# Linear attention in front of a low-rank mixer: transposes by token halves, scores in one run, outputs on the whole array

## The chip, the cores and the metric

The kernel runs on one core of one Trainium2 chip. The metric is the device time of one execution in microseconds. The kernel before was timed three times: 671.49, 671.64 and 671.76 us, median 671.64 us.

## What is computed

Two blocks, one after the other. The first is linear attention with decay ("lightning attention") over 4 batches, 8 heads, 768 tokens and 64 dimensions; the second is a mixer on its output.

```python
# attention, by blocks of tokens (block = 64 in the reference)
intra = einsum('bhic,bhjc->bhij', qb, kb) * Dmask        # Dmask[i,j] = lam**(i-j) for i >= j
intra = einsum('bhij,bhjd->bhid', intra, vb)
inter = einsum('bhid,bhde->bhie', qb * lam_pow, kv_state)
out   = intra + inter
kv_state = lam**block * kv_state + einsum('bhsd,bhse->bhde', kb * rev_pow, vb)
# x = out as (batch, tokens, 512), then the mixer
h = x.transpose(0, 2, 1) @ U @ V                         # U: 768 x 32, V: 32 x 768
u = x + h.transpose(0, 2, 1)
y = u + maximum(u @ w_ch1, 0) @ w_ch2                    # w_ch1: 512 x 2048, w_ch2: 2048 x 512
```

All is fp32. The reference's block of 64 tokens is a way to write the sum; the kernel uses blocks of 128, which gives the same result.

## The kernel before

The tokens are cut into 24 steps (`NS`) of 128 tokens, six (`NT`) to a batch. A step `s` has number `c = s % NT` in its batch. The kernel has two parts: a front, in which attention and the mixing over tokens are done step by step, and the two large products (`hidden`, L719 to 749, and `product`, L857 to 870), which take u in 512-token groups. The front ends at about 119 us in the profile.

What one step of the front does on TensorE (PE):

- `prep` (L360) with `turn_half` (L347): q and k of 128 tokens arrive as 128 tokens x 8 heads x 64. Four transposes each on the whole 128x128 array bring them to "two heads x 64 dimensions" on the partitions and tokens along the row. ScalarE (ACT) copies each set of four from PSUM (L358). Step 0 does this in two parts.
- `scores` (L394): per head, k times q over 64 dimensions, for 128 x 128 tokens. Heads of a pair sit on the lower and upper 64 partitions, so two row tiles (64x128) work side by side; after step 6 (`s > NT`) the key tokens are halved as well, and four 64x64 tiles work side by side.
- `masked` (L405): VectorE (DVE) multiplies the scores by the decay mask, in two instructions of 128x512, into `sm`.
- `intra` (L446): the masked scores times v, per head, by halves of the tokens on 128x64 column tiles, into `px`; then ACT copies `px` to `x_nat` (L459).
- `inter` (L431): q scaled by GpSimd (POOL, L383) times the state `kv`, on 64x64 tiles, into the same `px`. It opens the sum in `px`, except at the first step of a batch, which has no state.
- `state` (L411): scaled k (POOL, L372) times v on 128x64 tiles into `pkv`; DVE adds the faded state (L426). The last step of a batch has none.
- `low` (L464): after the six steps of a batch, x times U on 128x32 tiles; `low_rows` (L477) splits the result into a part with few bits and its rest.
- `mix` (L512): seven steps later (`done = s - NT - 1`), one 512-column product adds the mixed part; DVE adds it to x (L518).
- `turn` (L523): four transposes of u for the large products. DVE splits them (L537 and L548), a closure `turned` in the next step does the rest on ACT (L551) and POOL (L552). The u tile itself is stored to HBM from here (L535) for the residual at the end.

The order of all this is written out by hand in the list `pieces` (L562 to 584), and the tile framework is told to keep it (`manual_schedule`). In one pass of the loop for step `s`, TensorE gets: q and k transposes of step `s + 1`, `mix(done)`, `low` if a batch has ended, `intra(s)`, `state(s)`, `scores(s + 1)`, `inter(s + 1)`, and `turn(done)`. Weight steps for the large products (`aside`, `late`) are set among them on DVE, ACT and the DMA queue of SyncE. q, k and v are loaded ahead, into three or four buffers each, as soon as a step has let go of one (`load_next`).

PSUM in the front has eight banks: one each for `pq`, `pk`, `pt` and `pu`, two for the scores and two for `px`. `pkv` uses the bank of `pk`, the output transposes that of `pt`, the mix and the first low-rank product that of `pu`.

An fp32 matmul stands in the trace as two records (two passes, each with its own weight load); a transpose and a matmul of the float32r type as one.

Of the kernel before, what the change touches and what calls it, by code (L numbers as in the profile page):

```python
# [18 lines left out]
def kernel(  # L19
# [319 lines left out]
    def keep_busy(n):  # L339

        out = one_bank([P, C], "idle", "pq")
        for i in range(n):
            nc.tensor.matmul(out=out[:, 0:P], lhsT=blank, rhs=blank, start=True, stop=True)  # L343

    qts, kts = {}, {}

    def turn_half(s, a0, name):  # L347

        ts, tag = (qts, ("pq", "pt")) if name == "q" else (kts, ("pk", "pu"))
        if a0 == 0:  # L350
            ts[s] = att.tile([P, HP, P], FP32, tag=name + "t", bufs=2, name=name + "t")
        n = HP // parts(s)
        pt = one_bank([P, n, P], "p" + name, tag[a0 > 0])
        for a in range(a0, a0 + n):
            nc.tensor.transpose(  # L355
                out=pt[:, a - a0, :], in_=raw[s, name][:, 2 * a : 2 * a + 2, :], identity=ident
            )
        nc.scalar.copy(ts[s][:, a0 : a0 + n, :], pt)  # L358

    def prep(s):  # L360
        for a0 in range(0, HP, HP // parts(s)):
            for name in "qk":
                turn_half(s, a0, name)
        st[s].update(qt=qts.pop(s), kt=kts.pop(s))
        for name in "qk":
            load_next(name)
# [27 lines left out]
    def scores(s):  # L394
        qt, kt = st[s]["qt"], st[s]["kt"]
        st[s]["pss"] = pss = two_banks("pss", "pss").rearrange("p x (a i) -> p x a i", a=HP)
        for a in range(HP):
            for x in range(2):
                for rows in half if s > NT else [slice(0, P)]:
                    nc.tensor.matmul(  # L400
                        out=pss[rows, x, a, :], lhsT=kt[half[x], a, rows],
                        rhs=qt[half[x], a, :], start=True, stop=True,
                    )

# [6 lines left out]
    def state(s):  # L411
        c = s % NT
        if c < NT - 1:
            ks, vr = st[s]["ks"], raw[s, "v"]
            pkv = one_bank([P, HP, D], "pkv", "pk")
            for a in range(HP):
                for x in range(2):
                    nc.tensor.matmul(  # L418
                        out=pkv[half[x], a, :], lhsT=ks[:, a, x, :], rhs=vr[:, 2 * a + x, :],
                        start=True, stop=True,  # L420
                    )
            kv[s + 1] = att.tile([P, HP, D], FP32, tag="kv", bufs=2, name="kv")
            if c == 0:
                nc.vector.tensor_copy(out=kv[s + 1], in_=pkv)
            else:
                nc.vector.tensor_tensor(out=kv[s + 1], in0=pkv, in1=st[s]["faded"], op=ALU.add)  # L426
        del st[s]
        del raw[s, "v"]
        load_next("v")

    def inter(s):  # L431

        st[s]["px"] = both = two_banks("px", "px")
        px = both[:, :, 0 : HP * D].rearrange("p x (a e) -> p x a e", a=HP)
        if s % NT == 0:
            return

        for a in range(HP):
            for x in range(2):
                for t in range(2):  # L440
                    nc.tensor.matmul(  # L441
                        out=px[half[t], x, a, :], lhsT=st[s]["qs"][half[x], a, half[t]],
                        rhs=kv[s][half[x], a, :], start=(a == 0), stop=False,
                    )

    def intra(s):  # L446
        first = s % NT == 0
        sm, vr, px = st[s]["sm"], raw[s, "v"], st[s]["px"]
        px = px[:, :, 0 : HP * D].rearrange("p x (a e) -> p x a e", a=HP)
        for a in range(HP):  # L450
            for x in range(2):
                for t in range(2):
                    nc.tensor.matmul(  # L453
                        out=px[half[t], x, a, :], lhsT=sm[:, x, a, half[t]],
                        rhs=vr[:, 2 * a + x, :], start=(first and a == 0), stop=(a == HP - 1),
                    )
        pool, tag = (att, "x10") if s % 10 == 5 else (x_pool, "x")
        xs[s] = pool.tile([P, C], FP32, tag=tag, name="x_nat")
        nc.scalar.copy(xs[s].rearrange("p (a x e) -> p x a e", a=HP, x=2), px)  # L459


    pps = {}

    def low(b):  # L464

        tag = "pq" if b else "pu"
        pp = one_bank([P, P], "pp", tag) if b < B - 1 else bank([P, P], "pp", "b2")
        for c in range(NT):
            for g in range(G):
                nc.tensor.matmul(  # L470
                    out=pp[g * R : (g + 1) * R, :], lhsT=u_w[:, c, :],
                    rhs=xs[b * NT + c][:, g * P : (g + 1) * P],
                    start=(c == 0), stop=(c == NT - 1),
                )
        pps[b] = pp

    def low_rows(b):  # L477
# [3 lines left out]
        own = [(slice(g * R, (g + 1) * R), slice(g * P, (g + 1) * P)) for g in range(G)]  # L481
        if b == 0:

            rows_f = tmp("p_f")[0:R]
            for rows, cols in own:
                nc.scalar.copy(rows_f[:, cols], pp[rows])
            own = [(slice(0, R), slice(0, C))]
            pp = rows_f
        for rows, cols in own:
# [19 lines left out]
    def next_of_low(b):  # L509
        pps[b].pop(0)()  # L510

    def mix(s):  # L512
        b, c = divmod(s, NT)
        pu = one_bank([P, C], "pu", "pu") if s < NS - NT - 1 else bank([P, C], "pu", "b2")
        nc.tensor.matmul(  # L515
            out=pu, lhsT=v_hl[:, c * P : (c + 1) * P], rhs=p_hl, start=True, stop=True
        )
        nc.vector.tensor_tensor(out=xs[s], in0=pu, in1=xs[s], op=ALU.add)  # L518

    uhl, ud, turned = {}, {}, {}  # L520
    hl_at, d_at = [hl_pool], [d_pool]

    def turn(s):  # L523
# [5 lines left out]
        cols = slice(n * P, (n + 1) * P)  # L529
        pt = one_bank([P, CT, P], "put", "pt") if g < FG else bank([P, CT, P], "put", "b1")  # L530
        for ct in range(CT):
            nc.tensor.transpose(  # L532
                out=pt[:, ct, :], in_=xs[s][:, ct * P : (ct + 1) * P], identity=ident
            )
        nc.sync.dma_start(out=u_d[s], in_=xs.pop(s))  # L535
        t = tmp("ut").rearrange("p (c n) -> p c n", n=P)
        nc.vector.tensor_scalar(t.bitcast(U32), pt.bitcast(U32), HI, None, ALU.bitwise_and)  # L537
        hi, low, diff = uhl[g][:, 0, :, cols], uhl[g][:, 1, :, cols], ud[g][:, :, cols]
        if g >= FG:

            nc.vector.scalar_tensor_tensor(diff, t, 1.0 + E, pt, ALU.mult, ALU.subtract)
# [5 lines left out]

        nc.vector.tensor_tensor(out=low, in0=pt, in1=t, op=ALU.subtract)  # L548

        def rest():  # L550
# [3 lines left out]
            )  # L554

        turned[s] = rest

    pieces = [("prep", 0), ("scale", 0), ("scores", 0), ("inter", 0), ("masked", 0)]  # L562
    for s in range(NS):
        b, c = divmod(s, NT)
        done = s - NT - 1
        more = s + 1 < NS
        step = [("prep", s + 1), ("scale", s + 1)] * more + [("fade", s)] * (c == 1)
        step += [("late", s - 1)] * (s in (NT, 3 * NT - 1))
        step += [("mix", done)] * (0 <= done < NS - NT - 1)
        step += [("low", b - 1)] * (c == 0 and b > 0)  # L570
        step += [("low_rows", b - 1)] * (c == 0 and b > 0)
        step += [("intra", s)]
        step += [("next_of_low", b - 1)] * (c == 0 and b > 0)
        step += [("late", s)] * (s < NT - 1 or s == NT) + [("state", s)]
        step += [("next_of_low", b - 1)] * (c == 0 and b > 0)
        step += [("turned", done - 1)] * (done > 0) + [("late", s)] * (done >= 0)
        step += [("next_of_low", b - 1)] * (c == 0 and b > 0)
        step += [("scores", s + 1)] * more
        step += [("aside", s)] * (s >= 2 * NT)
        step += [("inter", s + 1), ("masked", s + 1)] * more  # L580
        step += [("fade", s + 1)] * (more and c > 0)
        step += [("aside", s)] * (s < 2 * NT)
        step += [("turn", done)] * (done >= 0 and done // TG < FG)
        pieces += step
    waiting = {name: list(range(NS)) for name in "qkv"}

    def load_next(name, engine=nc.sync):
# [6 lines left out]
        "intra": intra, "state": state,  # L594
        "low": low, "low_rows": low_rows, "next_of_low": next_of_low, "mix": mix, "turn": turn,
        "scale": scale, "turned": lambda s: turned.pop(s)(),
    }
# [77 lines left out]
    for name in "qkv":  # L675
        load_next(name)
    make_identity(nc, ident)
    keep_busy(2)
    pl = one_bank([P, H], "pl", "pt")
    nc.tensor.matmul(out=pl, lhsT=lam_row[:, H:], rhs=lam_row[:, 0:H], start=True, stop=True)  # L680
# [289 lines left out]
```

## Time and profile before

| What | Value |
|---|---|
| median of 3 runs | 671.64 us |
| the profiled execution's own time | 671.76 us |
| its span on the core | 669.9 us |
| q and k transposes, L355 | 192 records, 284 and 279 ns mean |
| scores on 64x128 tiles, L400 | 112 records, 305 ns mean |
| scores on 64x64 tiles, L400 | 544 records, 276 ns mean |
| outputs, L453, on 128x64 tiles | 768 records, 225 ns mean |
| state, L418 | 320 records, 222 ns mean |
| state's part, L441 | 640 records, 220 ns mean |
| output transposes in all, L532 | 96 records, 282 ns mean |
| mix in all, L515 | 24 records, 451 ns mean |
| masking, L409 on DVE | 48 instructions, 685 ns mean |

How to read it: a record's length holds its latency, and matmuls overlap in the pipeline, so the mean of one is not what one costs. What counts is the distance from the start of one row of the timeline to the start of the next. The clock of TensorE is granted in full after the opening.

The shapes in a row of the profile are "tile rows * tile columns" and then the moving operand, "partitions x elements".

### The profile page before, as it was taken

What the parts mean: (1) busy time and instruction counts of PE and PEld (TensorE: products, weight loads), DVE (VectorE), ACT (ScalarE), POOL (GpSimd) and SP (SyncE); (2) the same over time, 40 slices, a digit from 0 to 9 for tenths busy, and PEclk for the clock granted to TensorE, in tenths of its full rate; (3) what the DMA queues carried; (4) which work ended last, traced back from release to release, by engine and by line L of the source; (5) the groups of instructions that cost most, each with busy time, mean ns of one, the idle gap of its engine ahead of it and who ended that gap; (6) DMA issues with size and microseconds to landing.
All of it is one profiled execution on the core that took longest, in us unless ns stands there. A gap on an engine that the chain in (4) does not pass through costs nothing.

```text
span 669.9 us, 13328 instructions
## 1 busy us (share of the span) xinstructions
PE 663.9 (99%) x5204; PEld 544.5 (81%) x5204; DVE 497.5 (74%) x873; ACT 277.5 (41%) x517; POOL 112.1 (17%) x92
## 2 busy tenths in 40 slices
PE   9999999999999999999999999999999999999997
PEld 8898989788888888888888888888888888888886
DVE  4689989877999777777797265787586775865864
ACT  4675866454655444444454122232322322322320
POOL 4455767240000000000000000030030300300300
PEclk9999999999999999999999999999999999999999
DMA  8999894354776655555577989854363353543421
GB/s 188 219 234 248 212 246 141 102 196 153 262 251 233 215 202 202 201 202 204 204 282 273 326 308 392 282 184 136 95 220 95 118 196 95 160 155 94 163 90 63
DMA packets 131776, 131.29 MB, mean 196 GB/s; under 512 B 81346, under 2 KB 89794, under 8 KB 131714
## 3 DMA queue, kind: packets, MB, share of 16 engines
q1 hardware_dynamic: 130512, 130.05, 61.1%
q8 instruction: 41, 0.67, 0.4%
q10 hardware_dynamic: 1202, 0.39, 0.2%
q14 instruction: 21, 0.17, 0.1%
HBM read 80.09 MB, written 50.33 MB: 195 GB/s over the span
## 4 chain that ended last, share of the span: by engine, by line
PE 97%; DVE 1%; DMA 1%; ACT 0%; issue 0%; DVEq 0%; ACTq 0%
PE pz L733 27%; PE pz L868 13%; PE pz L866 13%; PE pd L743 13%; PE pd L870 13%; PE px L453 4%; PE pss L400 3%; PE put L532 2%; PE pq L355 2%; PE pkv L418 1%; PE pk L355 1%; PE px L441 1%; DMA qraw<-in_q_dram 1%; PE pp L470 1%; PE pu L515 1%; PE idle L343 0%
## 5 line engine op out<-in xcount | busy, mean ns | idle before, releaser
L733 PE MATMUL pz<-u_hl,w 128*128 128x512 f32 x768 | 190.5, 397 | 0.0
L733 PEld LDWEIGHTS pz<-u_hl,w 128*128 128x128 f32 x768 | 144.0, 188 | 35.4 <-issue 0.4
L868 PE MATMUL pz<-w_hl,m 128*128 128x512 f32 x384 | 151.1, 396 | 0.0
L866 PE MATMUL pz<-w_hl,m 128*128 128x512 f32 x384 | 150.9, 396 | 0.0
L870 PE MATMUL pd<-w_d,m 128*128 128x512 f32 x384 | 149.5, 396 | 0.0
L849 ACT ACTIVATE m<-mt 128x512 fp32r<-128x512 f32 x96 | 60.5, 632 | 196.4 <-PE pd L870 140.9
L850 DVE SCALAR_TENSOR_TENSOR m<-rm,m 128x512 fp32r<-128x512 f32 x96 | 71.4, 746 | 53.8 <-ACT m L849 53.5
L895 POOL TENSOR_TENSOR o<-o,u 128x512 f32<-128x512 f32 x20 | 29.9, 1527 | 447.4 <-DVE o L891 447.4
L748 DVE SCALAR_TENSOR_TENSOR r<-pd,r 128x512 f32<-128x512 f32 x96 | 61.8, 686 | 53.6 <-ACT r L739 43.5
L743 PE MATMUL pd<-u_d,w 128*128 128x512 f32 x384 | 98.6, 397 | 0.0
L739 ACT ACTIVATE r<-pz 128x512 f32<-128x512 f32 x96 | 52.2, 596 | 93.2 <-PE pz L733 92.5
L868 PEld LDWEIGHTS pz<-w_hl,m 128*128 128x128 f32 x384 | 72.3, 188 | 17.7
L870 PEld LDWEIGHTS pd<-w_d,m 128*128 128x128 f32 x384 | 72.3, 188 | 17.6
L866 PEld LDWEIGHTS pz<-w_hl,m 128*128 128x128 f32 x384 | 72.3, 188 | 17.6
L743 PEld LDWEIGHTS pd<-u_d,w 128*128 128x128 f32 x384 | 72.1, 188 | 17.3
L851 DVE SCALAR_TENSOR_TENSOR m<-m 128x512 fp32r<-128x512 f32 x96 | 69.1, 721 | 0.9
L848 DVE TENSOR_SCALAR mt<-rm 128x512 uint32<-128x512 uint32 x96 | 46.1, 481 | 26.4 <-DMA rm<-r_d 26.1
L409 DVE TENSOR_TENSOR sm<-pss,mask 128x512 f32<-128x512 f32 x48 | 30.9, 685 | 7.3 <-PE pss L400 7.1
L212 ACT CAST w<-wt 128x512 fp32r<-128x512 f32 x32 | 19.9, 620 | 30.6 <-DVE wt L209 23.4
L383 POOL TENSOR_TENSOR qs<-qt,powq 128x512 f32<-128x512 f32 x20 | 25.9, 1297 | 20.3 <-ACT qt L358 19.8
L453 PEld LDWEIGHTS px<-vraw,sm 128*64 128x64 f32 x768 | 24.6, 137 | 5.5 <-issue 2.3
L453 PE MATMUL px<-vraw,sm 128*64 128x64 f32 x768 | 28.1, 225 | 0.1
(88 smaller groups left out, 682.1 us busy)
## 6 DMA issues: line engine op xcount, KB each, us to landing
r_d<-r SPq DMA_DIRECT2D x96, 256.0 KB, 2.4
rm<-r_d SPq DMA_DIRECT2D x96, 256.0 KB, 2.7
words<-in_moe_w_ch_dram SPq DMA_DIRECT2D x30, 512.0 KB, 4.5
w_d<-w SPq DMA_DIRECT2D x16, 768.0 KB, 3.3
w_hl<-w_d SPq DMA_DIRECT2D x16, 512.0 KB, 6.3
vraw<-in_v_dram SPq DMA_DIRECT2D x24, 256.0 KB, 5.0
u_d<-x_nat SPq DMA_DIRECT2D x24, 256.0 KB, 3.7
u<-u_d SPq DMA_DIRECT2D x24, 256.0 KB, 4.0
```

Of the source, the lines that this page charges most:

```text
L453: nc.tensor.matmul(out=px[half[t], x, a, :], lhsT=sm[:, x, a, half[t]], rhs=vr[:, 2 * a + x, :], start=(first and a == 0), stop=(a == HP - 1),
L733: nc.tensor.matmul(out=acc[g][0], lhsT=w[:, n, ct, :], rhs=uhl[g][:, n, ct, :], start=(ct == 0 and n == 0), stop=(ct == CT - 1 and n == 1),)
L739: nc.scalar.mul(rs[g], acc[g][0], 4096.0 + 1.0)
L743: nc.tensor.matmul(out=acc[g][1], lhsT=w[:, 2, ct, :], rhs=ud[g][:, ct, :], start=(ct == 0), stop=(ct == CT - 1),)
L748: nc.vector.scalar_tensor_tensor(rs[g], acc[g][1], 4096.0, rs[g], ALU.mult, ALU.add)
L848: nc.vector.tensor_scalar(t.bitcast(U32), r.bitcast(U32), HI, None, ALU.bitwise_and)
L849: nc.scalar.activation(out=m[:, 0], in_=t, func=AF.Relu)
L850: nc.vector.scalar_tensor_tensor(m[:, 1], r, 0.0, hi, ALU.max, ALU.subtract)
L851: nc.vector.scalar_tensor_tensor(m[:, 2], hi, E, low, ALU.mult, ALU.subtract)
L866: nc.tensor.matmul(out=pz, lhsT=m[:, 0, cols], rhs=hl[:, 0], start=first, stop=False)
L868: nc.tensor.matmul(out=pz, lhsT=m[:, 1, cols], rhs=hl[:, 1], start=False, stop=end)
L870: nc.tensor.matmul(out=pd, lhsT=m[:, 2, cols], rhs=dd, start=first, stop=end)
```

## The change

- q, k and output transposes take 64 tokens at a time: stationary 64 x 128, moving the 64 x 64 identity, on the two row tiles of a 64x128 arrangement, whose results go to two banks. q and k share one PSUM tile of two banks (`pqk`), which `pkv` uses too.
- Scores always run on 64x128 tiles, and stand directly before the next transposes.
- Outputs (`intra`) run per head on the whole array, 128 tokens at once, first the four even heads, then the four odd ones. They stand behind the mix, which is cut in two runs of 256 columns. Outputs now open the sum in `px`.
- State's part (`inter`) comes after `intra(s)` and `state(s)` of its own step, and the copy of `px` to `x_nat` after it.
- `turn` takes the u of the step before (`done - 1`) and shares two banks (`pm`) with the mix of `done`; its splitting on DVE (`split`) and the addition of the mix (`mixed`) are pieces of their own behind both; the store of u is one too, at the end of the step.
- `low` stands right behind the scores at the end of its batch, in the banks of `px`, and ACT copies its result out at once in the first three batches.

The order in a pass of the loop on TensorE becomes: q and k transposes of `s + 1`, `turn(done - 1)`, `mix(done)`, `intra(s)`, `state(s)`, `inter(s)`, `scores(s + 1)`, and `low` where a batch ends.

```diff
-    def turn_half(s, a0, name):
+    def turn_parts(s, a0):
...
+        pt = two_banks("pqk", "px" if a0 else "pqk")[:, :, 0 : 2 * n * D]
+        pt = pt.rearrange("p t (n a i) -> p t n a i", n=2, a=n)
+        for i, name in enumerate("qk"):
+            for a in range(n):
+                for t in range(2):
+                    nc.tensor.transpose(
+                        out=pt[:, t, i, a, :],
+                        in_=raw[s, name][half[t], 2 * (a0 + a) : 2 * (a0 + a) + 2, :],
+                        identity=ident[half[t], half[t]],
+                    )
+        for i, ts in enumerate((qts, kts)):
+            nc.scalar.copy(
+                ts[s][:, a0 : a0 + n, :].rearrange("p a (t i) -> p t a i", t=2), pt[:, :, i]
+            )
...
     def scores(s):
...
-                for rows in half if s > NT else [slice(0, P)]:
-                    nc.tensor.matmul(
-                        out=pss[rows, x, a, :], lhsT=kt[half[x], a, rows],
-                        rhs=qt[half[x], a, :], start=True, stop=True,
-                    )
+                nc.tensor.matmul(
+                    out=pss[:, x, a, :], lhsT=kt[half[x], a, :], rhs=qt[half[x], a, :],
+                    start=True, stop=True,
+                )
...
+    def intra(s):
+
         st[s]["px"] = both = two_banks("px", "px")
         px = both[:, :, 0 : HP * D].rearrange("p x (a e) -> p x a e", a=HP)
+        sm, vr, alone = st[s]["sm"], raw[s, "v"], s % NT == 0
+        for x in range(2):
+            for a in range(HP):
+                nc.tensor.matmul(
+                    out=px[:, x, a, :], lhsT=sm[:, x, a, :], rhs=vr[:, 2 * a + x, :],
+                    start=(a == 0), stop=(alone and a == HP - 1),
+                )
+
+    def inter(s):
+
+        px = st[s]["px"][:, :, 0 : HP * D].rearrange("p x (a e) -> p x a e", a=HP)
+        for a in range(HP if s % NT else 0):
             for x in range(2):
                 for t in range(2):
                     nc.tensor.matmul(
                         out=px[half[t], x, a, :], lhsT=st[s]["qs"][half[x], a, half[t]],
-                        rhs=kv[s][half[x], a, :], start=(a == 0), stop=False,
+                        rhs=kv[s][half[x], a, :], start=False, stop=(a == HP - 1),
                     )
...
     def low(b):
...
+        pp = two_banks("pp", "px")[:, 0, 0:P] if b < B - 1 else bank([P, P], "pp", "b2")
...
+        pps[b] = rows_f = tmp("p_f")[0:R]
+        for g in range(G):
+            nc.scalar.copy(rows_f[:, g * P : (g + 1) * P], pp[g * R : (g + 1) * R])
...
     def mix(s):
         b, c = divmod(s, NT)
+        weights = v_hl[:, c * P : (c + 1) * P]
+        if s < NS - NT - 1:
+            pm = both_halves(s)[:, :, 2 * P :]
+            for x in range(2):
+                nc.tensor.matmul(
+                    out=pm[:, x], lhsT=weights, rhs=p_hl[:, x * 2 * P : (x + 1) * 2 * P],
+                    start=True, stop=True,
+                )
+            return
...
+    def mixed(s):
+        pm, x = pms.pop(s)[:, :, 2 * P :], xs[s].rearrange("p (x e) -> p x e", x=2)
+        nc.vector.tensor_tensor(out=x, in0=pm, in1=x, op=ALU.add)
...
     def turn(s):
...
+        pt = both_halves(s + 1)[:, :, 0 : 2 * P].rearrange("p t (c i) -> p t c i", i=D)
+        for ct in range(CT):
+            for n in range(2):
+                nc.tensor.transpose(
+                    out=pt[:, n, ct, :], in_=xs[s][half[n], ct * P : (ct + 1) * P],
+                    identity=ident[half[n], half[n]],
+                )
+        del xs[s]
...
     for s in range(NS):
         b, c = divmod(s, NT)
         done = s - NT - 1
         more = s + 1 < NS
-        step = [("prep", s + 1), ("scale", s + 1)] * more + [("fade", s)] * (c == 1)
+        turns = done > 0 and (done - 1) // TG < FG
+        mixes = 0 <= done < NS - NT - 1
+        step = [("prep", s + 1), ("scale", s + 1)] * more
+        step += [("turn", done - 1)] * turns + [("mix", done)] * mixes
+        step += [("fade", s)] * (c == 1)
         step += [("late", s - 1)] * (s in (NT, 3 * NT - 1))
-        step += [("mix", done)] * (0 <= done < NS - NT - 1)
-        step += [("low", b - 1)] * (c == 0 and b > 0)
-        step += [("low_rows", b - 1)] * (c == 0 and b > 0)
-        step += [("intra", s)]
+        step += [("split", done - 1)] * turns + [("mixed", done)] * mixes
+        step += [("intra", s), ("state", s), ("inter", s)]
         step += [("next_of_low", b - 1)] * (c == 0 and b > 0)
-        step += [("late", s)] * (s < NT - 1 or s == NT) + [("state", s)]
+        step += [("late", s)] * (s < NT - 1 or s == NT)
         step += [("next_of_low", b - 1)] * (c == 0 and b > 0)
         step += [("turned", done - 1)] * (done > 0) + [("late", s)] * (done >= 0)
         step += [("next_of_low", b - 1)] * (c == 0 and b > 0)
         step += [("scores", s + 1)] * more
+        step += [("low", b)] * (more and c == NT - 1)
         step += [("aside", s)] * (s >= 2 * NT)
-        step += [("inter", s + 1), ("masked", s + 1)] * more
+        step += [("masked", s + 1)] * more
+        step += [("low_rows", b)] * (more and c == NT - 1)
         step += [("fade", s + 1)] * (more and c > 0)
         step += [("aside", s)] * (s < 2 * NT)
-        step += [("turn", done)] * (done >= 0 and done // TG < FG)
+        step += [("store", done)] * (done >= 0 and done // TG < FG)
         pieces += step
```

Also changed: the opening's idle matmuls and the product that spreads lam use other banks (`pm` and `pss`), and the two DVE instructions of `split` read and write the halves of the tokens in their own order.

## The prediction

> **What bounds the kernel now.** I read the head of the page first, then the windows view by stage, the waits of TensorE's matmuls, the timeline of one step, and the weight loads grouped by shape.
>
> ```profile
> PE 663.9 (99%) x5204; PEld 544.5 (81%) x5204; DVE 497.5 (74%) x873; ACT 277.5 (41%) x517; POOL 112.1 (17%) x92
> ...
> PE   9999999999999999999999999999999999999997
> ```
>
> TensorE is busy from end to end, so only what shortens or lengthens its own queue counts, unless another engine stops it. The windows view of the front (columns: length, then each engine's busy time, granted clock, DMA share):
>
> ```profile
> 35.00:63.50 28.50, 27.90 (x736) 25.37 (x729) 24.41 (x40) 20.18 (x49) 16.63 (x14) 1.00 0.99 240
> 63.50:93.40 29.90, 29.77 (x755) 26.70 (x753) 27.63 (x50) 21.17 (x48) 19.83 (x16) 1.00 0.93 230
> 93.40:119.00 25.60, 25.60 (x698) 23.46 (x698) 23.88 (x44) 15.97 (x38) 17.30 (x14) 1.00 0.61 159
> ```
>
> The front ends at 119 us. VectorE (third busy time) is nearly full too, and the DMA engines up to 63 us: TensorE binds, with little room below. The waits view names only this for TensorE's matmuls from 5 to 119 us:
>
> ```profile
> PE put L532 <- DVE x_nat L518: 0.6, 1, 0.6
> PE pq L355 <- DMA qraw<-in_q_dram: 0.2, 1, 0.2
> ```
>
> One step of the front on TensorE (start, length, tile rows*columns, moving shape, records; an fp32 matmul leaves two records, a transpose one):
>
> ```profile
> 73.36 0.66 PE L532 MATMUL put<-ident,x_nat 128*128 128x128 f32 x4
> 73.85 0.60 PE L355 MATMUL pq<-ident,qraw 128*128 128x128 f32 x4
> 74.28 0.60 PE L355 MATMUL pk<-ident,kraw 128*128 128x128 f32 x4
> 74.64 0.47 PE L515 MATMUL pu<-vp 128*128 128x512 f32 x1
> 75.04 1.15 PE L453 MATMUL px<-vraw,sm 128*64 128x64 f32 x32
> 76.03 0.64 PE L418 MATMUL pkv<-vraw,ks 128*64 128x64 f32 x16
> 76.59 1.10 PE L400 MATMUL pss<-qt,kt 64*64 64x128 f32 x32
> 77.52 0.64 PE L441 MATMUL px<-kv,qs 64*64 64x64 f32 x32
> 78.09 0.66 PE L532 MATMUL put<-ident,x_nat 128*128 128x128 f32 x4
> ```
>
> Distances between starts give paces. Transposes: 0.43 / 4 = 109 ns each. Outputs: 0.98 for 16 pairs of records (two column tiles side by side), 58 ns a pair and 0.05 left over. State: 0.57 for 8 pairs, 58 each, 0.10 left over. Scores: 0.92 for 8 groups of four tiles, 109 each and 0.05. State's part: 0.58 for 8 groups of four, 58 each. The leftovers are the changes of tile shape: 0.10 when the old shape ends, then one exposed weight load. In the early steps, whose scores already run on 64x128 tiles, that row starts at 24.32 and the next at 25.41: 1.09 = 8 pairs x 111.6 ns + 0.20, so a 128-column load costs 0.10 after a change, and a 64-column one 0.05. Into transposes: 0.10 + 0.06 (at 26.04 and 26.10 two loads start 0.06 apart).
>
> [...]
>
> ```profile
> L515 PEld LDWEIGHTS pu<-vp 128*128 128x128 f32 x24 | 4.5, 189 | 0.5
> L453 PEld LDWEIGHTS px<-vraw,sm 128*64 128x64 f32 x768 | 24.6, 137 | 5.5 <-issue 2.3 <-DVE sm L409 1.4 <-DVE ut L537 1.0
> L470 PEld LDWEIGHTS pp<-x_nat,u_w 128*32 128x32 f32 x192 | 5.0, 110 | 1.3 <-ACT qt L358 0.7 <-issue 0.5
> ```
>
> From 64 to 128 columns +52 ns, from 32 to 64 +27: about 0.82 ns a column, so 128 columns occupy the loader 0.82 x 128 = 105 ns. [...]records of 137 ns follow each other at 58. [...]
>
> **The change, part by part**, TensorE first.
>
> *q and k transposes.* Eight of 109 ns become 16 with 64 tokens each, stationary 64x128, moving 64 columns, on two row tiles that run in pairs as the early scores do. Streaming halves to 55; the load of a transpose takes 0.06. I take 60 ns a pair; bounds 55, and 120 if the halves go in turn. Steps 1 to 23: 23 x 8 x (109 - 60) = -9.0 us. *Output transposes*, 16 steps: 16 x 4 x 49 = -3.1.
>
> *Mix*: one 512-column matmul (0.235, the pace of the same form in the large products: 3.75 / 16) becomes two of 256: 0.224; 17 times, -0.2.
>
> *Outputs* (intra). Sixteen matmuls in 128x64 pairs become eight on the whole array: the same 16 paces of 64 streamed columns, but each now loads 128 columns where two tiles loaded 64 side by side. Streaming takes 53, loading 105. Is a pace then set by the load? One place shows it. Half-speed opening, fp32, 128 columns loaded, only 8 streamed; the first record alone, then both:
>
> ```profile
> 2.20 0.38 PE L680 MATMUL pl<-lam_row 1*128 1x8 f32 x1
> ...
> 2.20 0.59 PE L680 MATMUL pl<-lam_row 1*128 1x8 f32 x2
> ```
>
> The ends lie 0.21 apart, as far as those of L343 beside it, which streams 128 columns ((1.44 - 0.58) / 4 = 0.215 from its five records). So the load sets the pace, and 0.21 at half speed (transposes 0.21 apart at 5 us, 0.109 later) is 107 at full speed. I take 109; bounds 58 (all hidden) and 112. 24 steps x 16 x (109 - 58.4) = +19.4 us: the largest term.
>
> *Scores*: 17 steps go from 109 to 111.6: +0.3. *State, state's part*: same tiles, 0.
>
> *Changes of shape.* Before, a late step has three: into outputs 0.145, scores 0.15, transposes 0.165; an early one has four, 0.66. After: scores and both transposes share 64x128, then mix and outputs 128x128 (0.20[...]), state 128x64 (0.145), state's part 64x64 (0.15), scores (0.20): 0.70. Over the front, with the three low-rank products, about 12.4 before and 16.3 after: +3.9; bounds +1.5 (the mix's load is not exposed) and +5.
>
> Late step: 12 x 0.060 + 0.224 + 1.744 + 0.467 + 0.467 + 0.893 + 0.70 = 5.22 against 4.75 for the same sum before (4.74 in the timeline). TensorE's sum: -9.0 - 3.1 - 0.2 + 19.4 + 0.3 + 3.9 = +11.3.
>
> *Waits.* Outputs need the masked scores. Scores to outputs was state's part, transposes, mix: 2.4 us; it becomes 0.72 + 0.43 = 1.15 late, 0.48 + 0.20 = 0.68 early. VectorE starts 0.32 after the last score's start and takes 0.69 for the first half, which is all that the first four outputs need now: about 1.07, so late steps just fit and steps 0 to 5 wait 0.4: +2.4, less 0.3 that step 0 waits already. Queued behind the waiting outputs are state, state's part and the next scores. After the first low-rank product four ScalarE copies (about 0.3 each, estimated from 0.26 for a faded copy of 64 columns) must leave the two banks that outputs want: +0.6. ScalarE now waits for state's part before it copies outputs, and behind that stand the 2^-12 copy, fading (1.06), then q and k copies, on which state waits for its banks: it fits by 0.2, and where weight steps put 0.6 to 1.2 more in, three times, about +1.2 in all. VectorE does the same work in a longer step: its stall at 60.59 to 62.30 (scores' slot 1.71 instead of 0.92) mostly goes, -0.5, the q wait goes, -0.3; what is late next is the masking, as above. Sum +3.1; I take +2.5, bounds 0 and +9.
>
> Nothing moves on the DMA queue: q, k, v, weights and u stores stand in the same order, a store still last in its step. GpSimd's scaled q is now needed half a step later. Past 119 us nothing changes, TensorE is full to the end, so all of it reaches the end.
>
> Profiled execution 671.76 (span 669.9 and 1.9 around it) + 11.3 + 2.5 = 685.5; it lies 0.1 above the median: 685.3.
>
> **Rivals.** *A, faster: loads hide.* If an output pass on the whole array keeps 58 ns, the 19.4 falls away: TensorE -8.1 + 2.5. But early steps gain nothing (3.94 + 0.4 against 4.29), DMA is 0.99 full to 63 us, and VectorE has 29.90 - 27.63 + 25.60 - 23.88 = 4.0 free afterwards; a gain of some 2.7 is left: 669. It decides below a pace of 58.4 + (19.4 - 13.8) / 0.384 = 73 ns. Against it: L680. *B: halves go in turn.* 120 ns for two halves: 12.1 lost and 2.7 on top, less waiting (-2): 698. For: no transpose here runs on a part of the array. Against: row tiles run beside each other in the early scores. *C: the masking stops every step.* With VectorE late by 0.4 in the 17 late steps, +6.8: 692. For: its lag from the last score is 0.7 to 1.0 in steps with weight work. Against: the longer step frees it.
>
> **Numbers.** About 0.2% can be told from no change. Likeliest (679 to 690) 0.74, A 0.08, C 0.12, B 0.06. Range 679 to 693: low from hidden mix loads (-2.4), an output pace of 105 (-1.5) and no waits (-2.5); high from C. Faster 0.08, same 0.02, slower 0.90.
>
> **What would show it.** Outputs' row of 16 records taking 1.7 us or more, loads near 188 ns; late steps of 5.2 us; transposes at 60 ns a pair, 0.48 for q and k; four shape changes; outputs waiting for masked scores in steps 0 to 5 alone. Wrong if the outputs' row stays near 0.95 or transposes stay at 0.87.

## The result, and the profile after

The kernel with the change takes 689.7 us in the median of four executions (687.75, 688.42, 690.99, 691.55), the kernel before beside it 671.57 us. The ratio is 1.027, with a 95% interval of 1.0236 to 1.0305: slower by 2.7%. The forecast was 685.3 us, in a range of 679 to 693: the side and the range hold, and the point is 4.4 us too low.

The profile is of the execution that took 690.99 us (span 689.2). The head of its page:

```profile
PE 679.4 (99%) x4821; PEld 562.9 (82%) x4821; DVE 498.9 (72%) x861; ACT 278.6 (40%) x525; POOL 111.7 (16%) x92
```

TensorE has 383 records fewer and is busy 15.5 us longer; its share is 99% as before, so this line alone doesn't tell work from waits. The first product of the large kind starts at 138.43 us, before it was 118.99: 19.4 us. The span grew by 19.3. All of the loss arises in the front. The windows view of the front (length, then each engine's busy time, granted clock, DMA share, GB/s):

```profile
42.50:75.70 33.20, 31.42 (x622) 29.30 (x618) 24.68 (x38) 20.87 (x49) 17.15 (x14) 1.00 0.75 186
75.70:108.40 32.70, 32.04 (x644) 30.05 (x636) 26.11 (x44) 21.43 (x50) 19.98 (x17) 1.00 0.82 206
```

Before, VectorE had 2.3 us to spare in the window from 63.5 to 93.4 and the DMA engines were 0.93 to 0.99 full to there. Now VectorE has 8.5 and 6.6 us to spare in these two windows (33.20 - 24.68, 32.70 - 26.11) and the DMA engines about a fifth: neither binds. TensorE, which stood for 0.1 us between 63.5 and 93.4, now stands for 1.8 and 0.7 us (33.20 - 31.42, 32.70 - 32.04). So the front is longer chiefly because TensorE has more to do, and next because it waits. One late step shows what it does (timeline of TensorE: start, length, tile, moving shape, records):

```profile
91.77 0.41 PE L358 MATMUL pqk<-ident,qraw 64*128 64x64 f32 x8
...
92.95 1.89 PE L443 MATMUL px<-vraw,sm 128*128 128x64 f32 x16
94.78 0.69 PE L424 MATMUL pkv<-vraw,ks 128*64 128x64 f32 x16
...
97.01 0.41 PE L358 MATMUL pqk<-ident,qraw 64*128 64x64 f32 x8
```

The step takes 97.01 - 91.77 = 5.24 us; 5.22 was forecast. By distances between starts, of these rows and of those between: q and k transposes 0.49 (0.245 for four pairs, 61 ns a pair; 60 was taken), output transposes 0.35, mix 0.34, outputs 1.83, state 0.61, state's part 0.63, scores 0.99. Outputs can be read as 16 x 107 ns and the 0.10 at a change of shape that the forecast reckoned with; inside the row the records start 112 ns apart. Before, they took 0.99. The loads of its outputs, in the groups of weight loads by shape from 4 to 139 us (busy, mean ns of one):

```profile
L443 PEld LDWEIGHTS px<-vraw,sm 128*128 128x128 f32 x384 | 47.0, 199 | 3.2 <-ACT faded L399 0.9 <-ACT sc L168 0.9 <-ACT p_f L480 0.7
```

An output's load of 128 columns lasts 199 ns (the tiled one of before lasted 137), and there is one to each 64 streamed columns.

Early steps hold the waits of the forecast. The timeline of all engines in step 3, of which the masking and the outputs are shown:

```profile
26.39 1.29 DVE L415 TENSOR_TENSOR sm<-pss,mask 128x512 f32<-128x512 f32 x2 [1.22 <-PE pss L406]
...
27.19 1.08 PE L443 MATMUL px<-vraw,sm 128*128 128x64 f32 x8 [0.34 <-issue]
```

The masking's first half ends 0.69 after 26.39, at 27.08, and outputs start at 27.19, after 0.34 us of standing still. The bracket says "issue"; in the next step the same 0.35 is put down to ACT's L399. The releaser is taken to be the one whose end fits, the masking on VectorE. A wait that the forecast did not have comes once in each batch, before the first mix of its rows:

```profile
79.06 0.58 ACT L460 COPY x_nat<-px 128x512 f32<-128x512 f32 x1 [0.99 <-PE px L443]
...
81.46 0.61 ACT L505 CAST vp<-vp 32x512 fp32r<-32x512 f32 x1
...
82.13 0.51 PE L525 MATMUL pm<-vp 128*128 128x256 f32 x2 [0.66 <-ACT vp L505]
```

The mix needs the low part of the product's rows, which VectorE forms at L496 and ScalarE spreads at L505. ScalarE had no gap from 79.06, when it began to copy the outputs, to 82.07: two casts, the split of u and L505 follow the copy. The mix, whose transposes were through at 81.4, starts at 82.13. The kernel before has the same chain on ScalarE, and just as long:

```profile
66.77 0.58 ACT L459 COPY x_nat<-px 128x512 f32<-128x512 f32 x1 [2.21 <-PE px L453]
...
69.16 0.62 ACT L505 CAST vp<-vp 32x512 fp32r<-32x512 f32 x1
```

From 66.77 to 69.78 it is 3.01 us, as it is from 79.06 to 82.07. What shrank is TensorE's work between the end of the outputs and the mix: 3.35 us before (66.55 to 69.90, where the mix starts without a wait), 2.45 now (78.95 to 81.40). The next step's state's part (0.57) stood there before and stands behind the mix now, and the transposes take 0.84 instead of 1.29.

And the opening ran at half pace for longer than before. The start of the front in this execution:

```profile
8.74 3.68 PE L443 MATMUL px<-vraw,sm 128*128 128x64 f32 x16
12.35 1.12 PE L424 MATMUL pkv<-vraw,ks 128*64 128x64 f32 x16
```

Outputs take 3.6 us where a late step takes 1.83, state 1.05 (to 13.40) instead of 0.61. Full pace comes at about 17.5 us; before, it was there by 9. The granted clock in the page shows 9 in these slices as everywhere; the last section says why.

### The profile page after: what moved, and what is told of

It reads as the page before. It is cut to its first block, busy times and chain, and to the rows that moved or that the text cites. A ratio compares the mean times of both kernels' runs of the same rounds, so it can differ in the third digit from the quotient of the medians.

```text
span 689.2 us, 12534 instructions
## 1 busy us (share of the span) xinstructions
PE 679.4 (99%) x4821; PEld 562.9 (82%) x4821; DVE 498.9 (72%) x861; ACT 278.6 (40%) x525; POOL 111.7 (16%) x92
## 4 chain that ended last, share of the span: by engine, by line
PE 96%; ACT 1%; DVE 1%; DMA 1%; issue 1%; ACTq 0%; DVEq 0%
PE pz L778 26%; PE pz L913 13%; PE pz L911 13%; PE pd L788 13%; PE pd L915 13%; PE px L443 6%; PE pss L406 3%; PE px L454 2%; PE pkv L424 2%; PE pqk L358 1%; PE pm L525 1%; PE pp L470 1%; DMA kraw<-in_k_dram 1%; PE put L555 1%; PE pm L573 0%
## 5 line engine op out<-in xcount | busy, mean ns | idle before, releaser
L443 PE MATMUL px<-vraw,sm 128*128 128x64 f32 x384 | 48.6, 282 | 2.1 <-ACT faded L399 0.7
L443 PEld LDWEIGHTS px<-vraw,sm 128*128 128x128 f32 x384 | 47.0, 199 | 3.2 <-ACT faded L399 0.9
L415 DVE TENSOR_TENSOR sm<-pss,mask 128x512 f32<-128x512 f32 x48 | 30.9, 686 | 16.3 <-PE pss L406 16.2
L460 ACT COPY x_nat<-px 128x512 f32<-128x512 f32 x24 | 14.0, 585 | 44.1 <-PE px L454 39.5
```

What stands on the lines that cost most here:

```text
L443: nc.tensor.matmul(out=px[:, x, a, :], lhsT=sm[:, x, a, :], rhs=vr[:, 2 * a + x, :], start=(a == 0), stop=(alone and a == HP - 1),)
```

## The experiments

The theory: outputs on the whole array are bound by their weight loads. The rivals: they are bound by something else in the whole-array form (streaming, or the banks), so that more streamed columns would cost; or the loss is in waits and in the order, and tiled outputs would not bring it back. Behind each median stand the range of the executions, the ratio to the kernel before, and its 95% interval.

**Outputs by halves again**, the rest of the change kept:

```diff
-                nc.tensor.matmul(
-                    out=px[:, x, a, :], lhsT=sm[:, x, a, :], ...
+                for t in range(2):
+                    nc.tensor.matmul(
+                        out=px[half[t], x, a, :], lhsT=sm[:, x, a, half[t]], ...
```

> The changed kernel with one part undone: outputs by halves of the tokens on 128x64 column tiles again, all else as changed. Theory (weight loads of 128 columns set the pace of the outputs on the whole array): the outputs' slot falls from 1.82 to about 1.0 us, late steps to about 4.4 to 4.7 us (VectorE and the DMA queue then near full), time about 668 to 673. If the theory that a half-speed opening comes from load-bound outputs holds as well, TensorE reaches its full pace near 9 us as in the kernel before, not near 17, and the time is at the low end. Rival (the loss lies in the waits and shape changes, outputs cost the same on either tile): time stays above 683.

Measured: 673.32 us (13 executions, 672.46 to 674.74), 1.0032 of the kernel before (1.0022 to 1.0042). That is just above the 668 to 673 expected. The outputs' row falls to 1.00:

```profile
86.00 1.15 PE L444 MATMUL px<-vraw,sm 128*64 128x64 f32 x32
87.00 0.69 PE L424 MATMUL pkv<-vraw,ks 128*64 128x64 f32 x16
```

One line of the change holds nearly the whole loss. But what is left of the change gains nothing: it is 0.3% slower, though its late step is 4.50 us where that of before is 4.74. Its waits view, TensorE's matmuls from 4 to 125 us (in all, times, longest):

```profile
PE pm L527 <- ACT vp L507: 2.1, 3, 1.0
PE pqk L358 <- DVE kv L432: 1.4, 2, 1.0
```

These two and the next two, of 0.8 and 0.7, make 5.0 us, where the same view of before had 0.8 in two: the gain of the shorter transposes is given back here and, as I read it, in the changes of shape.

**Whole-array outputs alone**, put into the kernel before (the edit is the reverse of the one above):

> The kernel before with one part of the change alone: outputs on the whole array, at their old place in the order; all else as before. Theory (pace 107 instead of 58.4 ns for 16 passes in 24 steps): +18.7 us and no more shape changes than before (the change into column tiles moves from ahead of the outputs to behind them), about 689 to 692; more by some 4 if the opening stays at half pace. Rival (whole-array outputs save a shape change and cost nothing): 668 to 672.

Measured: 690.14 us (689.17 to 690.65), 1.0281 (1.0251 to 1.0312).

The outputs' row takes 1.82 us (from 92.02 to the state's start at 93.84) in another order and beside other transposes: the cost belongs to the form of the outputs, not to their place. Alone it costs 19 us, the forecast's 19.4.

**Twice the columns streamed** by seven of eight outputs; the second half of each result is not used:

```diff
-                    out=px[:, x, a, :], lhsT=sm[:, x, a, :], rhs=vr[:, 2 * a + x, :],
+                    out=px2[:, x, a, 0:wide, :], lhsT=sm[:, x, a, :],
+                    rhs=vr[:, 2 * a + x : 2 * a + x + wide, :],
```

> The changed kernel with seven of the eight output matmuls of a step streaming 128 columns (the v of two heads) where they streamed 64; the second half of each result is not used. Loads stay as they are. Theory (a load of 128 columns sets the pace at 107 ns, streaming is hidden below it): the outputs' slot stays within 0.1 us of 1.82, time within 3 us of the changed kernel (687 to 693)[...]. Rival (streaming and load add up, or streaming sets the pace): the slot grows by 14 x 53 ns = 0.75 us, time about 706 to 709.

Measured: 688.14 us (687.52 to 689.94), 1.026 (1.0231 to 1.0288).

```profile
89.50 1.89 PE L444 MATMUL px<-vraw,sm 128*128 128x128 f32 x16
91.33 0.69 PE L424 MATMUL pkv<-vraw,ks 128*64 128x64 f32 x16
```

128 columns cost what 64 do: 1.83 us. (The 53 ns for 64 streamed columns, here and in the forecast, is an estimate: a quarter of the 0.215 us that the opening's idle products, of 128 columns, took at half pace in the profile before.) So it isn't the streaming of 64 columns that sets the pace, and that rival is dead. What is left is the load, whose mean length of 199 ns against 137 goes with it, or some other fixed price of a whole-array fp32 pass: no run loads fewer columns on the whole array, so these two aren't parted.

**Two idle products** behind the first scores, to hasten the opening, which stayed at half pace until about 17.5 us in the profile of the change:

```diff
-    pieces = [("prep", 0), ("scale", 0), ("scores", 0), ("masked", 0)]
+    pieces = [("prep", 0), ("scale", 0), ("scores", 0), ("masked", 0), ("warm", 2)]
```

> The changed kernel with two idle fp32 matmuls added on TensorE behind the first scores, before the second step's transposes; nothing else. Theory (the opening stays at half pace until about 17 us[...]): full pace is reached before the first outputs, near 9 us, and the time falls by 3 to 4.5 us to about 685 to 687. Rival (the slow opening is a wait on data, or pace comes at a fixed time): no gain, or up to 0.9 us lost for the two matmuls, 689 to 691.

Measured: 693.06 us (688.47 to 693.92), 1.0315 (1.0273 to 1.0357): no gain, as the rival had it, and two us more loss than it allowed. In the profiled execution, of 693.92, the half pace stayed until 18 us: step 0's outputs took 3.60. Two products took 1.15 us of the queue and brought no pace. Another 1.5 us of this execution, whose mean granted clock is 0.997, was lost in mid-kernel, where step 7 takes 6.73 us from outputs to outputs instead of 5.24 (the last section).

**The change once more**, unaltered:

> The changed kernel once more, unaltered, for the pace of its opening. Theory (an execution whose TensorE is at full pace before 10 us takes about 688, one that stays at half pace to about 17 us takes about 691; which one happens differs from execution to execution): times spread from about 687.5 to 691.5, and the profiled execution's outputs of step 0 take 1.8 to 2.0 us if its own time is near 688, 3.6 us if it is near 691. Rival (the spread has nothing to do with the opening): the profiled time and the slot of the first outputs do not go together.

Measured: 688.1 us (687.51, 687.74, 688.1, 688.22, 691.49), 1.0249 (1.0229 to 1.0269). The profiled execution took 687.74 us and opens so:

```profile
8.91 2.21 PE L443 MATMUL px<-vraw,sm 128*128 128x64 f32 x16
11.05 0.69 PE L424 MATMUL pkv<-vraw,ks 128*64 128x64 f32 x16
```

Full pace at about 9.4 us. From outputs to outputs, steps 0 and 1 take 4.75 and 5.14 us here, 7.58 and 5.72 in the profile above: 3.4 us, and the two executions differ by 3.25. Each later step agrees within 0.02. So what parts these two is the opening's pace alone, and the times of this kernel near 688 and near 691 are read as the two lengths of it. Only two of the nine executions were profiled, and the kernel before, whose profile opens at full pace by 9 us, spreads over 3.3 us too (670.24 to 673.51 in 23 executions), with no profile to say why.

**Eight idle products** (`("warm", 8)` in the same place):

> The changed kernel with eight idle fp32 matmuls, not two, behind the first scores: some 3.4 us more of a full stream at half pace, 1.7 at full. Theory[...]: the pace doubles within the idle matmuls, the first outputs take 1.8 to 1.9 us in every execution, time about 689 to 691 with little spread. Rival (the full pace is a matter of time since the start, or of data): it comes near 17 us again and the time is 693 to 696.

Measured: 691.24 us (690.78 to 691.4), 1.0286 (1.027 to 1.0302).

```profile
8.06 1.16 PE L343 MATMUL idle<-blank 128*128 128x128 f32 x4
9.06 1.50 PE L343 MATMUL idle<-blank 128*128 128x128 f32 x12
```

They take 2.43 us of the queue (the next row starts at 10.49; the 3.4 and 1.7 us of the expectation are estimates, sixteen records of some 0.215 and 0.107 us), and step 0's outputs run at full pace. All four times lie within 0.6 us, where those of the unaltered change spread over 4, as the theory had it. But the profile doesn't show that the products brought the pace: it came at 9.06, after four of their sixteen records, and in the unaltered kernel at 9.4 without any. Nor do the four times mean four equal openings. The profiled execution (691.27) lost 1.5 us in mid-kernel, told in the last section, and its mean granted clock is 0.997; the other three have 0.999 and 1.000 and take as long, so they lost about as much in some other place, which no profile shows. The products earn nothing either way.

**Twice the columns streamed in step 0 alone** (`wide = 2 if s == 0 and ...`; again the second half is not used):

> The changed kernel with 128 streamed columns in the outputs of step 0 alone (seven of eight matmuls; the second half of each result is not used). Theory[...]: full pace from about 9 us on, first outputs 1.9 us, times 687.5 to 689 and no execution at 691. Rival (the opening is decided elsewhere): same spread as the unaltered kernel, 687.5 to 691.5.

Measured: 688.94 us (687.9 to 690.31), 1.0255 (1.0238 to 1.0271). The profiled execution had step 0's outputs in 3.22 us, partly at half pace, and the full one by 12.7. No time lies at 691, but the spread is 2.4 us: between the two theories. (The slowest, 690.31, has a mean granted clock of 0.997 as well.) This doesn't show whether the streaming of step 0's outputs has to do with the opening's pace.

**The spread early, ahead of the outputs.** Low part and spread move up in ScalarE's and VectorE's queues; first with outputs by halves, then with the change as it is:

```diff
+        step += [("next_of_low", b - 1)] * (2 * (c == 0 and b > 0))
         step += [("intra", s), ("state", s), ("inter", s)]
-        step += [("next_of_low", b - 1)] * (c == 0 and b > 0)
         step += [("late", s)] * (s < NT - 1 or s == NT)
-        step += [("next_of_low", b - 1)] * (c == 0 and b > 0)
+        step += [("next_of_low", b - 1)] * (c == 0 and b > 0)
         step += [("turned", done - 1)] * (done > 0) + [("late", s)] * (done >= 0)
-        step += [("next_of_low", b - 1)] * (c == 0 and b > 0)
```

> The changed kernel with outputs by halves on 128x64 tiles as in the first experiment, and the two first pieces behind the low-rank product (ScalarE's spreading of the high part, VectorE's low part) put ahead of the outputs in their step, the third ahead of the 2^-12 copy. Theory (the mix of steps 7, 13 and 19 waits for ScalarE's last spread, which stands behind the copy of the outputs, and this is 2 to 3 us of what that kernel loses by waiting): these waits fall under 0.2 us each and the time falls from 673.3 to about 671, the kernel before or slightly below. Rival (DMA and VectorE bound that kernel anyway, the time comes back as other waits): 672.5 to 673.5.

Measured: 674.11 us (673.4 to 676.49), 1.0036 (1.0023 to 1.005); without the early spread it was 1.0032 (1.0022 to 1.0042). The profile is of the slowest execution, 676.49, two us above the next. The wait of the mix (2.1 us) is gone from its list, and this heads it:

```profile
PE pqk L358 <- DVE kv L430: 4.0, 3, 1.5
```

q and k transposes use the banks of the state (`pkv`), and VectorE, which has the low part ahead of it now, empties them later.

> The changed kernel (outputs on the whole array) with ScalarE's spreading of the high part and VectorE's low part put ahead of the outputs in the first step of a batch, and the third piece ahead of the 2^-12 copy. Theory (the wait of the mix for ScalarE's last spread in steps 7, 13 and 19, 2.2 us in the trace, is real and came with the order of the change): that wait goes, VectorE has room in the longer steps, and the time falls by about 2 us against the unaltered kernel (688.1 to about 686). Rival (the wait only moves to the transposes, which need the bank of the state, as in the kernel with outputs by halves): 688 again.

Measured: 689.34 us (686.72, 687.59, 688.29, 690.39, 693.74, 694.14), 1.0271 (1.0234 to 1.0308). The profile, of the 694.14, has the opening at half pace until 25 us, which costs steps 0 and 1 together 6.3 us against the 687.74 above. Past it, the steps in which the mix waited are shorter, by 0.48 between the outputs of steps 6 and 7 and by 0.68 between those of 18 and 19, and the one between steps 12 and 13 is longer by 0.66:

```profile
83.14 1.41 DVE L496 TENSOR_TENSOR vp<-p_f,p_h 32x512 fp32r<-32x512 f32 x1
...
85.07 0.47 PE L358 MATMUL pqk<-ident,qraw 64*128 64x64 f32 x8 [1.17 <-DVE kv L430]
```

VectorE's copy of the state (L430) starts at 84.59, when the low part (L496) is through, and the transposes start when the copy is. So the wait is real, and about half of what is won is lost again at the next engine in the line; a net half microsecond of steps is below what these six times can show.

**Whole-array transposes**, the rest of the change kept:

```diff
-                for t in range(2):
-                    nc.tensor.transpose(out=pt[:, t, i, a, :],
-                        in_=raw[s, name][half[t], 2 * (a0 + a) : 2 * (a0 + a) + 2, :], ...
+                nc.tensor.transpose(out=pt[:, i, a, :],
+                    in_=raw[s, name][:, 2 * (a0 + a) : 2 * (a0 + a) + 2, :], identity=ident)
```

> The changed kernel with all transposes of the front on the whole array again, at their new places in the order; all else as changed. Theory (a pair of half transposes takes 61 ns where one whole one takes 109): 23 x 8 + 16 x 4 = 248 transposes x 48 ns = 11.9 us more on TensorE, the same number of shape changes; the waits of outputs for masked scores in the first steps (about 2.1 us) and half of the mix's wait for ScalarE go in exchange, so about 697 to 699. Rival (halves do not pay, the transposes were hidden): within 2 us of 688.

Measured: 693.45 us (692.78 to 695.01), 1.0322 (1.0298 to 1.0347): 5.4 us above the change measured again, 6.8 between the two profiles' fronts (142.00 and 135.19), and below the 697 to 699 expected. A late step here:

```profile
92.06 0.66 PE L357 MATMUL pqk<-ident,qraw 128*128 128x128 f32 x4
...
97.82 0.66 PE L357 MATMUL pqk<-ident,qraw 128*128 128x128 f32 x4
```

5.76 us, so the halves bring 0.52 there. But early steps take 5.14 us with either form: with whole transposes nothing waits for the masking, and with halves the time that they save is the wait. In the early steps their gain is nil. The mix waits here only once, 0.4 us, instead of three times: whole transposes cover ScalarE's chain.

**Mixing added behind the state, spread early, outputs by halves**: both waits taken on together.

```diff
-        step += [("split", done - 1)] * turns + [("mixed", done)] * mixes
-        step += [("intra", s), ("state", s), ("inter", s)]
+        step += [("split", done - 1)] * turns
+        step += [("next_of_low", b - 1)] * (c == 0 and b > 0)
+        step += [("intra", s), ("state", s)]
         step += [("next_of_low", b - 1)] * (c == 0 and b > 0)
+        step += [("mixed", done)] * mixes + [("inter", s)]
```

> The changed kernel with outputs by halves (first experiment), VectorE's addition of the mix put behind the addition to the state, ScalarE's high spread ahead of the outputs and VectorE's low part ahead of the addition of the mix. Theory (that kernel loses 1.8 us to transposes that wait for the state's bank and some 2 us to mixes that wait for ScalarE): 670.5 to 672, level with the kernel before. Rival (VectorE and the DMA queue bound it): 673 again.

Measured: 673.86 us (672.83 to 674.87), 1.003 (1.0021 to 1.0039). The waits view now has at its head the transposes of the output, which wait for VectorE's addition (L538) 2.0 us in two, and the mix, which waits for the spread 1.0 in one; what waits for the state's banks is 0.8 in two. Each order moves the wait. Which engine binds with tiled outputs isn't shown: in this trace, of the 29.0 us from 67 to 96, TensorE is busy 27.6 and VectorE 25.8, and the DMA share is 0.99. None of these kernels is faster than the one before.

## Why the prediction held, and where it failed

Held against the execution of 687.74 us, whose opening is like that of before (front 135.19 - 118.99 = 16.2 us longer):

- *Outputs* (+19.4 forecast): the mechanism fits, by the doubled streaming at no cost, and by 19 us for this line alone. With 0.10 for the change of shape taken apart the pace is 107 ns, where 109 was taken: 24 x 16 x (107 - 58.4) = +18.7. The reading behind it, one matmul with 8 streamed columns in the opening, was enough to choose the sign.
- *Transposes*: 61 ns a pair against 60, on row tiles beside each other; rival B (halves in turn) is out. TensorE's own gain is -8.8 and -3.1, as forecast to 0.2. What reaches the end is less, 5.4 to 6.8 us: the waits below lie where it was made.
- *Changes of shape and the rest*: four in a step; late step 5.24 against 5.22. TensorE's work by measured paces comes to about +11.0, forecast +11.3.
- *Masking in the early steps* (0.4 each): five waits of 0.35, and none in late steps: rival C is out. *Copies of p_f* (0.6): 0.5. *ScalarE's copies before the state's banks* (1.2): by slots longer than their pace, about 0.6 (the step from 56.44 to 62.12 is 0.44 longer than its neighbours, the one after it 0.19).
- *Rival A* (loads hide) asked for a pace under 73 ns; it is 107 or more.

**The step that failed is "Waits"**, by its size. Its list came to +3.1, of which I took +2.5; the front's 16.2 less 11.0 of work leaves 5.2. The missing term is the mix, which waits for the spread of the low part and stood at nothing. The waits view of that execution:

```profile
PE pm L525 <- ACT vp L505: 2.2, 3, 0.9
PE px L443 <- issue: 0.9, 3, 0.3
PE px L443 <- ACT faded L399: 0.7, 2, 0.3
```

2.2 us in three steps; the second and third rows are mostly the masking under other names. I followed ScalarE's copies forward to the state's banks and did not follow the same queue to its other customer. The prediction saw that the order shortens the way from scores to outputs, and not that it shortens the way from outputs to the mix: 2.45 us against the 3.01 of ScalarE's chain, where it was 3.35. (In the first batch the low part itself is late as well: VectorE ends it at 44.86, behind a weight step.) Some 0.5 us more is the remnant of half pace in step 0 (outputs 2.14, not 1.82 or so). The early spread shows the wait real and in great part not recoverable.

The other part is what the prediction didn't consider at all: it took the opening's pace as fixed. By their times, two of the first four executions paid some 3.4 us for it. Together, +2.7 for the waits, -0.3 for the work and some 2 for the opening in the median make the 4.4. The experiments on the opening don't decide when the pace comes: two idle products brought none, with eight it came when it came without them (9.06 and 9.4 us), and with doubled streaming in step 0 it came at 12.24. The long openings were seen only with both transposes by halves and outputs bound by loads, in one profile of each kernel. The last section has the times from all the traces.

## What to carry to other kernels

Price an fp32 matmul by its form in a trace, and look at its load as well as at its stream: here 128 stationary and 64 moving columns cost 107 ns or more a pass, 128 moving columns cost no more (a row of 1.83 us with either), and two tiles side by side, each with a load of 64 columns, cost 58. A transpose needs its own price: by halves it has 128 stationary and 64 moving columns too, and a pair costs 61 ns (its loads last 139 ns, those of the outputs 192, in the profile of the 687.74). When a step is moved, follow its queue to every customer, not to the first; and a wait that is taken away where three engines are nearly full turns up at the next one. A gain in a stage that waits for another engine is no gain: look at which steps a shorter row would only wait in.

## What the runs showed of the hardware

Half pace is not only the opening's. In the profiles with two and with eight idle products it came back in mid-kernel, in the same step. With eight:

```profile
47.67 0.47 PE L525 MATMUL pm<-vp 128*128 128x256 f32 x2 [0.90 <-ACT vp L505]
```

The outputs that follow still run at full pace, 1.82 us (47.98 to 49.80). Then state takes 0.92, state's part 1.06 and scores 1.76 us instead of 0.61, 0.63 and 0.99; the step is 6.73 us long where the unaltered change has 5.24. That is 1.5 us of this execution's time. Here the granted clock shows it, in the windows view (the last three figures are the clock, the DMA share and GB/s):

```profile
46.58:49.99 3.41, 2.51 (x30) 2.33 (x28) 2.26 (x4) 2.75 (x7) 1.27 (x1) 1.00 1.01 242
49.99:53.40 3.41, 3.41 (x62) 3.17 (x61) 0.42 (x1) 1.48 (x5) 1.06 (x1) 0.50 0.51 130
```

The wait of 0.90 us alone doesn't explain it: both profiles of the unaltered change have the same wait before the same mix (at 48.89 and at 45.65) and keep their pace. What brought the half clock on isn't shown.

The traces' record of the granted clock goes further than the page of a profile. It begins only where the pace doubles: at 8.08 us in the kernel before, at 17.54 and 9.38 in the two profiles of the change, at 12.24 with doubled streaming in step 0, at 25.68 with the early spread. The views count what lies ahead of the record as full, so in the opening only the distances between starts tell half pace from full.

By those distances the full pace was there before 11 us in nine of the thirteen profiles. In four it came later: at 12.24, 17.54 and 25.68 us, as above, and between 18 and 19 us with two idle products. All four have transposes by halves and outputs on the whole array; but so have three of the nine, the change measured again, the one with eight idle products and the one with doubled streaming in every step. The six without one or the other, the kernel before among them, are all among the nine. So the two together went with every long opening and did not always bring one. Why the full pace comes when it does isn't shown.
